# Recurrent attention feeding a gated feed-forward: x of blocks 1 to 5 kept as f32, early loads without padding rows, planner recounted

## The chip, the cores and the metric

One core of one Trainium2 chip. The metric is the device time of one execution in microseconds (us), the median over the runs; lower is better. PE is the matmul engine (TensorE), DVE the vector engine, ACT the scalar engine, POOL the GpSimd engine, and SP the engine that issues nearly all DMA transfers. L1369 is line 1369 of the kernel before.

## The reference

```python
# r, k, v, w: [4, 8, 768, 48], u: [8, 48]
for t in range(S):
    cur = einsum('bhd,bhe->bhde', u[None] * kt, vt)
    y[:, :, t] = einsum('bhd,bhde->bhe', rt, state + cur)
    state = wt[:, :, :, None] * state + einsum('bhd,bhe->bhde', kt, vt)
x = y.transpose(0, 2, 1, 3).reshape(3072, 384)
h = x @ w_in                                   # [384, 2048]
g = where(h >= 1, h, where(h <= -1, 0, (h + 1) ** 2 / 4))
return g @ w_out                               # [2048, 384]
```

A linear attention with a decaying state gives x, and a feed-forward with a quadratic gate follows. All is f32.

## The kernel before, in words

The attention is done in 12 chunks of 256 tokens (u = 0 to 11), the feed-forward in six blocks of 512 tokens, so two chunks fill the x of a block. A matmul of f32 accuracy is made of three: each operand is split into a high and a low part (type fp32r), and three of the four products are summed. The 16 slices of the weights come packed and are unpacked for the first time during block 0 (POOL takes the sign, L485; DVE and ACT the rest, L481 to L490). Blocks 3 to 5 use fewer, combined products (the lines after L1000).

A chunk, in the names of the rows. `wq` holds the decay of half the channels, two tiles to a chunk and three tiles in turn; `rk` holds r and k of the same half, also two to a chunk and three in turn (rk_81, rk_82 and rk_83 are the three; wq_78, wq_79 and wq_80 likewise). Both have 128 rows, of which 2 x 48 carry data and 2 x 16 are padding that comes with the transfer. DVE scans the decay (`p`, L550, and `y` backwards, L545) and multiplies r and k by the scans (L571, L621). In the first three chunks (u < EARLY) ACT forms u*k (`nk`, L561), with u in four columns of the constants `cst`. PE multiplies r with u*k and with k inside groups of 32 tokens (`among`, L591, whose results DVE picks by a mask, L597), transposes k (L630), forms the update of the state (`umat`, L660; DVE adds it, L676 to L681), and puts y together in two runs of matmuls, `cross` and `along` (both L703). L591, L660 and L703 use 64x64 or 64x48 corners of the array; here they are called narrow, and the 128-row products L1369 (x @ w_in), L1389 and L1045 (g @ w_out) wide.

The result is evacuated into x. 48 data rows of 64 leave 16 free rows in each half, which the fourth part of the channels (`last`) fills by six small DMAs on SP (L827); chunks 0 and 1 do that by matmuls instead. In blocks 0 to 3 x is split while it is evacuated: ACT copies the high part (L781), DVE subtracts for the low part (L779). In blocks 4 and 5 (FLAT) ACT copies f32 into `xf` (L775), the six DMAs fill it, and `divided` splits a half block at once (ACT L1150, DVE L1152).

The order on every engine is made when the program is built. `op(engine, cost, due, reads, writes, emit)` records an operation with an assumed cost; `order()` lists them greedily by a key; `best()` tries several keys and keeps the order whose planned end is earliest; `kept_warm()` puts matmuls of zeros (`fill`, L439) where PE would idle, to hold its clock. `load` records a DMA, and `first=` fixes the place of the first ones in SP's queue.

Of the kernel before, what the change touches and what calls it, by code (L numbers as in the profile page):

```python
# [10 lines left out]
F32 = mybir.dt.float32  # L11
# [33 lines left out]
FLAT = {NB - 2, NB - 1}  # L45
# [5 lines left out]
USE, SPAN, COLUMN = 0.68, 3.4, 0.00168  # L51

EAGER, LATE = 16.0, 0.3
RISES = 7.0
COLD = 7.0
# [3 lines left out]
BACK, SHAKES, SHAKE, SEED = 4, 40, 0.7, 5  # L59
# [4 lines left out]
class Plan:  # L64
# [10 lines left out]
    BLOCK, FETCH = 256, 3.9  # L75
# [12 lines left out]
    def add(self, engine, cost, emit, due, reads=(), writes=(), port=False, size=0, fresh=True, first=None, grab=False, uses=(), drop=None, code=0):  # L88
# [6 lines left out]
        for x in writes:  # L95
# [3 lines left out]
                             fresh=fresh and engine == "PE", touch={*reads, *writes}, first=first, grab=grab, drop=drop, then=None, code=code,  # L99
# [19 lines left out]
    def best(self, steps, times):  # L119

        found = None
        for _ in range(ROUNDS):
            for op in self.ops:
                when, ahead = op["due"]
                op["key"] = times[when] - ahead
            order = self.order()
            end = max(self.end.values())
            if found is None or end < found[0]:
                found = end, order, (self.begin, self.end, self.given, self.extra)
            times = [self.begin[n] for n in steps]  # L130

        draw = random.Random(SEED)
        for n in range(SHAKES):
            if n % BACK == 0:
                self.begin, self.end, self.given, self.extra = found[2]
            for op, key in zip(self.ops, self.late()):
                op["key"] = key + draw.gauss(0.0, SHAKE) * (n % BACK == 0 < n)
            order = self.order()
            end = max(self.end.values())
            if end < found[0]:  # L140
                found = end, order, (self.begin, self.end, self.given, self.extra)
        self.begin, self.end, self.given, self.extra = found[2]
        for op in self.ops:
            op["touch"] |= {("b", self.given[n]) for n in op["uses"]}
        return found[1]
# [39 lines left out]
    def kept_warm(self, order, engine, banks, fill):  # L185

        ops, begin, end = self.ops, self.begin, self.end
        free, out, busy = 0.0, [], []
        used = {b: [n for n in order if b in ops[n]["touch"]] for b in banks}
        for n in order:  # L190
            op = ops[n]
            if op["e"] == engine:
                at = begin[n]
                use = sum(max(0.0, y - max(x, at - SPAN)) for x, y in busy)
                lack = at - free - (0.3 if at > EAGER else -LATE if free < COLD else 0.1)
                if at > EAGER:
                    lack = min(USE * SPAN - use, lack)
                if free and lack > 0.15:
                    for b in banks:
# [4 lines left out]
                            ops[m]["e"] == engine for m in (before, after)) and end[before] <= free  # L204
                        fresh = after is None or ops[after]["fresh"]
                        if held or fresh and at - max(0.0 if before is None else end[before], free) > (lack if at > EAGER else at - free - 0.3 - 1e-6):
                            out.append(lambda b=b, lack=lack, free=free, held=held: fill(b, lack, free, held))
                            busy.append((at - lack, at))
                            break
                free = at + op["cost"]  # L210
                busy.append((at, free))
            out.append(op["emit"])
        return out

    def order(self):
# [18 lines left out]
        issued = [(0, -99.0, 0.0)]  # L234

        def fetched(code):
            at = issued[-1][0] + code - self.BLOCK
            for had, t, each in reversed(issued):
                if had <= at:
                    return t + (at - had) * each + self.FETCH  # L240
            return 0.0
# [4 lines left out]
        def ready(n):  # L246
# [3 lines left out]
            if ops[n]["code"] > 64:  # L250
                t = max(t, fetched(ops[n]["code"]) - ops[n]["cost"])
# [6 lines left out]
        while any(open_.values()):  # L258
# [12 lines left out]
            assert t < never  # L271
            n = min((n for n in open_[e] if ready(n) <= t + 1e-9 and forced.get(e) in (None, n)),
# [1186 lines left out]
```

## Time and profile before

| | before |
|---|---|
| time, median of 3 runs | 501.33 us (500.96 to 502.52) |
| the profiled execution | 503.06 us, of which span 501.5 us |
| PE busy | 488.0 us, 97% of the span |
| DVE busy | 404.1 us, 81% |
| ACT busy | 312.7 us, 62% |
| POOL busy | 101.4 us, 20% |
| DMA | 54.30 MB, mean 108 GB/s |
| chain that ended last | PE 90%, DVE 4%, DMA 2%, issue 2%, ACT 1% |

The span is the recorded part of the execution; 1.56 us of the profiled execution lie around it. Busy is the time in which an engine had an instruction running. A busy PE isn't the same as a useful one: zero matmuls count too, and so do matmuls that drain slowly.

### The profile page before, as it was taken

How to read it: one execution, taken by the hardware profiler on the slowest of the kernel's cores; microseconds unless marked ns; L12 is line 12 of the kernel's file. 1: busy time of each engine (PE TensorE's matmuls, PEld its weight loads, DVE VectorE, ACT ScalarE, POOL GpSimd, SP SyncE). 2: the span in 40 equal slices, each digit the busy share in tenths (PEclk: the TensorE clock that was granted, in tenths of full speed). 3: DMA queues.
4: the chain of work that ended last, by engine and by line, in shares of the span. 5: the costliest groups of instructions: out<-in, count | busy, mean ns of one | idle time of the engine just before them, and what ended most of it. 6: DMA issues, size and time to landing. Idle time of an engine off the chain costs nothing.

```text
span 501.5 us, 13736 instructions
## 1 busy us (share of the span) xinstructions
PE 488.0 (97%) x5767; PEld 426.8 (85%) x5767; DVE 404.1 (81%) x702; ACT 312.7 (62%) x658; POOL 101.4 (20%) x80
## 2 busy tenths in 40 slices
PE   6979999999999999999999999999999999999996
PEld 4768988889999998888888788889899989898985
DVE  5899999988888898898999878779877675675573
ACT  4669799855555473765555656788866565465461
POOL 1656604530111111303031124432100000000000
PEclk9989999999999999999999999999999999999999
DMA  8984750522343434446153212222141000010002
GB/s 293 400 300 163 300 211 17 185 81 86 107 133 107 141 103 138 169 137 215 39 210 105 106 52 74 42 52 55 30 118 22 1 1 1 23 41 1 3 1 69
DMA packets 33286, 54.30 MB, mean 108 GB/s; under 512 B 15424, under 2 KB 22720, under 8 KB 33216
## 3 DMA queue, kind: packets, MB, share of 16 engines
q1 hardware_dynamic: 32784, 52.95, 31.9%
q8 instruction: 47, 0.77, 0.6%
q10 hardware_dynamic: 432, 0.39, 0.2%
q14 instruction: 23, 0.19, 0.1%
HBM read 47.04 MB, written 4.72 MB: 103 GB/s over the span
## 4 chain that ended last, share of the span: by engine, by line
PE 90%; DVE 4%; DMA 2%; issue 2%; ACT 1%; SPq 0%; DVEq 0%; ACTq 0%
PE h L1369 39%; PE acc L1389 20%; PE acc L1045 10%; PE bank L1045 9%; PE bank L703 4%; PE bank L591 3%; PE bank L630 2%; PE bank L660 1%; DMA cst<-in_consts 1%; DMA rk<-in_rk 1%; DVE fl L487 1%; PE bank L439 1%; PE acc L591 1%; DVE wt L490 1%; DVE y L545 0%
## 5 line engine op out<-in xcount | busy, mean ns | idle before, releaser
L1369 PE MATMUL h<-x,wt 128*128 128x512 f32 (+1 forms) x1035 | 220.1, 360 | 3.0 <-DVE x L779 2.9
L1369 PEld LDWEIGHTS h<-x,wt 128*128 128x128 f32 x1035 | 169.5, 189 | 31.7 <-DVE x L779 3.1
L1389 PE MATMUL acc<-gh,wt 128*128 128x256 f32 (+1 forms) x402 | 80.3, 335 | 0.0
L1389 PEld LDWEIGHTS acc<-gh,wt 128*128 128x128 f32 x402 | 60.9, 188 | 7.4
L1007 DVE SCALAR_TENSOR_TENSOR rk<-rk,h 128x512 f32<-128x512 f32 x48 | 32.8, 683 | 35.8 <-ACT rk L1006 34.2
L1178 ACT ACTIVATE g<-h 128x256 f32<-128x256 f32 (+1 forms) x67 | 31.9, 476 | 44.8 <-PE h L1369 40.6
L1004 ACT ACTIVATE rk<-h 128x512 f32<-128x512 f32 x48 | 28.6, 596 | 38.8 <-PE h L1369 38.8
L485 POOL TENSOR_SCALAR wraw<-fl 128x768 uint16<-128x768 f32 x13 | 41.8, 3224 | 51.4 <-ACT wraw L483 49.9
L1180 DVE SCALAR_TENSOR_TENSOR g<-g,h 128x256 f32<-128x256 f32 (+1 forms) x67 | 35.2, 529 | 14.4 <-ACT g L1179 12.4
L1389 PE MATMUL acc<-gl,wt 128*128 128x256 f32 (+1 forms) x201 | 44.5, 329 | 0.0
L1182 ACT CAST gh<-g 128x256 fp32r<-128x256 f32 (+1 forms) x67 | 32.7, 494 | 18.8 <-DVE g L1180 8.8
L617 POOL TENSOR_TENSOR r<-cst,d 128x512 f32<-128x512 f32 x18 | 20.2, 1143 | 99.8 <-PE bank L703 81.7
L1183 DVE TENSOR_TENSOR gl<-g,gh 128x256 fp32r<-128x256 f32 (+1 forms) x67 | 38.7, 589 | 0.8 <-ACT gh L1182 0.7
L1389 PEld LDWEIGHTS acc<-gl,wt 128*128 128x128 f32 x201 | 32.3, 188 | 4.0
L1179 ACT ACTIVATE g<-g 128x256 f32<-128x256 f32 (+1 forms) x67 | 34.4, 513 | 1.1
L550 DVE TENSOR_TENSOR_SCAN p<-wq,seeds 128x520 f32<-128x520 f32 x24 | 32.0, 1331 | 3.2 <-DMA wq<-in_w 2.3
L1006 ACT ACTIVATE rk<-rk 128x512 f32<-128x512 f32 x48 | 30.4, 634 | 0.9
L545 DVE TENSOR_TENSOR_SCAN y<-wq,seeds 128x520 f32<-128x520 f32 x24 | 29.8, 1242 | 0.8
L609 POOL TENSOR_TENSOR nk<-nk 128x768 f32<-128x768 f32 x9 | 17.3, 1920 | 61.4 <-DMA nk<-in_nk 37.9
L1013 DVE TENSOR_TENSOR gl<-rk,gh 128x512 fp32r<-128x512 f32 x36 | 25.5, 717 | 2.7 <-ACT gh L1012 2.4
L1013 DVE TENSOR_TENSOR g_again<-rk,nk_again 128x512 fp32r<-128x512 f32 x33 | 22.8, 701 | 5.8 <-ACT nk_again L1012 5.5
L1012 ACT CAST gh<-rk 128x512 fp32r<-128x512 f32 x36 | 22.1, 619 | 8.3 <-DVE rk L1007 4.7
(212 smaller groups left out, 914.5 us busy)
## 6 DMA issues: line engine op xcount, KB each, us to landing
rk<-in_rk SPq DMA_DIRECT2D x24, 512.0 KB, 5.3
wraw<-in_wbits SPq DMA_DIRECT2D x16, 768.0 KB, 7.5
nk<-in_nk SPq DMA_DIRECT2D x9, 768.0 KB, 4.7
wq<-in_w SPq DMA_DIRECT2D x24, 260.5 KB, 2.9
vn<-in_v SPq DMA_DIRECT2D x12, 384.0 KB, 6.8
last<-in_w SPq DMA_DIRECT2D x12, 256.0 KB, 3.0
out_y<-xf SPq DMA_DIRECT2D x15, 128.0 KB, 1.8
out_y<-g SPq DMA_DIRECT2D x6, 256.0 KB, 2.2
```

Source lines behind the costliest of these rows:

```text
L485: op(on, 0.62 if f in SIGNS else 3.2, due, [("fl", k)], [("raw", f)], lambda: e.tensor_scalar(out=half(1), in0=s, scalar1=0.0, scalar2=327 ...
L550: V.tensor_tensor_scan(out=pv[:, q].rearrange("p n c -> p (n c)"), data0=w[:, 0:SEG], data1=sv, initial=0.0, op0=ALU.mult, op1=ALU.add,)
L1007: op("DVE", 0.66, due, [("h", n)], [qk], lambda: V.scalar_tensor_tensor(out=gf, in0=gf, scalar=1.0, in1=bank[plan.given[hk]], op0=ALU.min, ...
L1013: op("DVE", 0.67, due, [key, ("h", i, k)], fresh_in(("l", i, k)), lambda: V.tensor_tensor(out=spare(k, 3 + i), in0=x, in1=spare(k, i).bitc ...
L1045: PE.matmul(bank[i][:, half * UT : half * UT + UT], lhsT=w[wi], rhs=g[gi], start=(b, i) not in opened, stop=True, skip_group_check=True)
L1178: op("ACT", c, due, [("h", n)], [("g", gk)], lambda: nc.scalar.activation(gs, hs(), AF.Relu, scale=0.5, bias=0.5), uses=[hk])
L1179: op("ACT", c, due, (), [("g", gk)], lambda: nc.scalar.activation(gs, gs, AF.Square))
L1180: op("DVE", 0.13 + 0.53 * k, due, [("h", n)], [("g", gk)], lambda: nc.vector.scalar_tensor_tensor(out=gs, in0=gs, scalar=1.0, in1=hs(), op ...
L1182: op("ACT", c, due, [("g", gk)], [("gh", gk)], lambda: nc.scalar.copy(ghs, gs))
L1183: op("DVE", 0.17 + 0.54 * k, due, [("g", gk), ("gh", gk)], [("gl", gk)], lambda: nc.vector.tensor_tensor(out=gls, in0=gs, in1=ghs.bitcast( ...
L1369: nc.tensor.matmul(hp, lhsT=wx[f][:, cs], rhs=xt[:, j, :], start=n == 0, stop=n == 8)
L1389: nc.tensor.matmul(o[j], lhsT=wx[f][:, cs], rhs=gt, start=first and i == 0, stop=stop and i == 2, skip_group_check=True)
```

## The change

- FLAT is now blocks 1 to 5, and `xf` stays at two tiles, taken in turn. Chunks 2 to 7 are evacuated by ACT alone, filled by six DMAs of 16 KB instead of 32 KB, and split by `divided`, which is recorded right behind the second chunk of the block.
- Early r and k (all six loads of the first three chunks) are sent as two transfers of 48 rows into tiles that DVE clears at the start (three MEMSETs of 128x1024, L541 of the new file); `wq` likewise, from the second load of a tile on.
- The four columns of u ride as two more columns of `wq` (523 instead of 521); `cst` shrinks to 128x192 and is loaded behind r and k instead of between them. `perm` is made on POOL instead of being loaded; the transfer of `us` waits for weight slice 5.
- The planner: other costs for the narrow matmuls, a price on going from narrow to wide (SWITCH) and a wish to keep narrow runs together (HOLD), an exact count of the instruction blocks that PE fetches, zero matmuls planned within the search, 12 shakes and 17 local ones (MOVES) in place of 40 shakes.

```diff
-FLAT = {NB - 2, NB - 1}
+FLAT = set(range(1, NB))
-USE, SPAN, COLUMN = 0.68, 3.4, 0.00168
+USE, SPAN, COLUMN = 0.68, 3.4, 0.00184
-BACK, SHAKES, SHAKE, SEED = 4, 40, 0.7, 5
+BACK, SHAKES, SHAKE, SEED = 4, 12, 0.7, 3
+MOVES = (521500, 587009, 888496, 283031, 12939, 164576, 355387, 922251, 331532, 701578, 205853, 500742, 732557, 367787, 559427, 662263,
...
-    xf = tiles(len(FLAT), [128, 3, WIDE], F32, "xf")
+    xf = tiles(2, [128, 3, WIDE], F32, "xf")
+    for i in range(3):
+        op("DVE", 0.6, (0, 200.0 - i), (), [("k", i), ("r", i)], lambda i=i: V.memset(rk[i], 0.0))
...
+    def rows_of(due, out, in_, keys, own, first):
+        if not own:
+            return load(due, out, in_, keys, first=first)
+        users = {n for key in keys for n in plan.readers.get(key, ())}
+        for h in range(2):
+            i = slice(HP * h, HP * h + D)
+            n = load(due, out[i], in_[i], [(*key, h) for key in keys], keys, first=first)
+            plan.ops[n]["deps"] |= users
...
-            load(due, wq[slot[q]], a["w"][u, q], [("w", slot[q])], first=rank(1 - q))
-            load(due, rk[slot[q]], a["rk"][u, q], [("k", slot[q]), ("r", slot[q])], first=rank(4 - 2 * q))
+            rows_of(due, wq[s], a["w"][u, q], [("w", s)], early and s in padded, rank(1 - q))
+            padded.add(s)
+            rows_of(due, rk[s], a["rk"][u, q], [("k", s), ("r", s)], early, rank(3 - q))
-            load(due, cst, a["consts"], ["cst"], first=3)
+            load(due, cst, a["consts"], ["cst"], first=4)
-                A.mul(ku[:, q, cs], rk[slot[q]][:, 1, cs], u_col[:, 2 * q + pr : 2 * q + pr + 1])
+                A.mul(ku[:, q, cs], rk[slot[q]][:, 1, cs], wq[slot[q]][:, SEG + 1 + pr : SEG + 2 + pr])
...
+        cost = op["cost"] + self.SWITCH * (op["small"] != was) + self.EVENT * op["code"]
...
             for u in ADDED.get(b, ()):
                 attention(u, *PULLED.get(u, (step_of(u), None)))
+                if u % 2 and u // 2 in FLAT and u // 2 < NB - 2:
+                    divided(u // 2)
```

How the orders move, at four places. First SP's queue at the start of the program, before:

```order
L419 DMA wq_78<-in_w 128x521
L419 DMA wq_79<-in_w 128x521
L419 DMA rk_81<-in_rk 128x1024
L419 DMA cst_67<-in_consts 128x196
L419 DMA rk_82<-in_rk 128x1024
L469 DMA wraw_143<-in_wbits 128x1536
L419 DMA vn_85<-in_v 128x2x384
L419 DMA below_71<-in_below 128x64
L469 DMA wraw_153<-in_wbits 128x1536
L419 DMA wq_80<-in_w 128x521
```

And the same place after the change (L529 is the line of `load` there, L579 the fetch of packed weights):

```order
L529 DMA wq_78<-in_w 128x523
L529 DMA wq_79<-in_w 128x523
L529 DMA rk_81<-in_rk 48x1024 x2
L529 DMA rk_82<-in_rk 48x1024 x2
L529 DMA cst_67<-in_consts 128x192
L579 DMA wraw_153<-in_wbits 128x1536
L529 DMA vn_85<-in_v 128x2x384
L529 DMA below_71<-in_below 128x64
L529 DMA wq_80<-in_w 128x523
L579 DMA wraw_163<-in_wbits 128x1536
```

`cst` has gone behind both tiles of r and k, and the third tile of the decay (wq_80) ahead of the second slice of weights.

DVE in the first chunk, before, from the multiplications of r and k to the first unpacking of weights:

```order
L571 TENSOR_TENSOR rk_82<-rk_82,y_87 128x512
L621 TENSOR_TENSOR rk_81<-rk_81,p_86 128x512
L621 TENSOR_TENSOR rk_82<-rk_82,p_86 128x512
L597 COPY_PREDICATED r_90<-cst_67,acc_111 128x512
L597 COPY_PREDICATED r_89<-cst_67,acc_110 128x512
L597 COPY_PREDICATED r_89<-below_71,acc_112 128x512
L597 COPY_PREDICATED r_90<-below_71,bank_115 128x512
L549 MEMSET seeds_73 128x8
L550 SCALAR_TENSOR_TENSOR p_86<-wq_80,seeds_73 128x520
L487 SCALAR_TENSOR_TENSOR fl_107<-fl_107,wraw_143 128x768
```

The same stretch after the change (order's name for the scan is SCALAR_TENSOR_TENSOR here):

```order
L701 TENSOR_TENSOR rk_82<-rk_82,y_87 128x512
L751 TENSOR_TENSOR rk_81<-rk_81,p_86 128x512
L751 TENSOR_TENSOR rk_82<-rk_82,p_86 128x512
L727 COPY_PREDICATED r_89<-cst_67,acc_110 128x512
L679 MEMSET seeds_73 128x8
L680 SCALAR_TENSOR_TENSOR p_86<-wq_80,seeds_73 128x520
L727 COPY_PREDICATED r_90<-cst_67,acc_111 128x512
L727 COPY_PREDICATED r_89<-below_71,acc_112 128x512
L727 COPY_PREDICATED r_90<-below_71,bank_115 128x512
L674 RECIPROCAL seeds_73<-p_86 128x8
```

The scan of the next chunk's decay (wq_80) has moved up between the first pick and the other three.

PE in chunk 4, before, at the end of the state's update:

```order
L660 MATMUL bank_117<-vn_85,kt_91 64x48 x2
L660 MATMUL h_114<-vn_85,kt_91 64x48 x2
L660 MATMUL bank_117<-vn_85,kt_91 64x48 x2
L660 MATMUL h_114<-vn_85,kt_91 64x48 x2
L1369 MATMUL h_113<-x_95,wt_898 128x256 x9
```

And after (L790 is `umat`, L833 `put`):

```order
L790 MATMUL bank_117<-vn_85,kt_91 64x48 x2
L790 MATMUL h_114<-vn_85,kt_91 64x48 x2
L790 MATMUL bank_117<-vn_85,kt_91 64x48 x2
L790 MATMUL h_114<-vn_85,kt_91 64x48 x2
L833 MATMUL bank_115<-rk_81,st_93 64x64
L833 MATMUL bank_116<-rk_81,st_93 64x64
```

`along` now follows `umat` with no wide product between them. The same holds in chunks 0, 1, 7 and 10; over the whole program the narrow runs that are followed by a wide product go from 39 to 34, and from 31 to 28 behind the first 60 us. Ahead of the first L721 no fill is left, and all fills together go from 22 rows with 5736 columns to 12 rows with 3509.

ACT behind the evacuation of chunk 3 (the second half of block 1), after the change (L1308, L1309 and L1312 are parts of the gate, L1280 the copy of `divided`):

```order
L1308 ACTIVATE g_97<-h_113 128x256
L1309 ACTIVATE g_97<-g_97 128x256
L1280 CAST x_95<-xf_109 128x3x256
L1308 ACTIVATE g_98<-h_114 128x256
L1309 ACTIVATE g_98<-g_98 128x256
L1312 CAST gh_100<-g_97 128x256
```

In the program before, chunk 3 had no such copy: x_95 was written by L781 and L779 straight from the bank. The copy now waits for the six DMAs, with the gates of the next products queued behind it.

## Rows read from the trace of the kernel before

**Rows 1.** Busy time of each engine in stretches of the span, instructions in brackets, then the granted TensorE clock (1.00 is full), the DMA share and the rate.

```profile
0.00:10.00 10.00, 5.23 (x35) 3.28 (x36) 5.28 (x9) 3.58 (x8) 2.23 (x14) 1.00 0.78 262
10.00:20.00 10.00, 10.00 (x280) 8.33 (x278) 8.03 (x12) 5.10 (x7) 5.01 (x2) 0.83 1.04 404
20.00:30.00 10.00, 7.00 (x40) 4.71 (x34) 9.82 (x16) 7.95 (x15) 6.28 (x3) 1.00 1.01 388
...
40.00:50.00 10.00, 10.00 (x250) 9.62 (x250) 9.89 (x17) 9.55 (x24) 6.16 (x2) 1.00 0.52 187
...
60.00:100.00 40.00, 40.00 (x381) 33.57 (x380) 37.46 (x55) 35.11 (x61) 15.57 (x6) 1.00 0.44 158
100.00:300.00 200.00, 200.00 (x3087) 174.07 (x3086) 174.47 (x309) 112.44 (x276) 35.62 (x26) 1.00 0.37 121
300.00:490.00 190.00, 189.60 (x1300) 169.34 (x1300) 135.88 (x252) 123.52 (x239) 19.94 (x26) 1.00 0.12 31
```

**Rows 2.** All waits of PE in the span: line, what it waited for, total us, times, longest us (two of five).

```profile
PE h L1369 <- DVE x L779: 2.9, 1, 2.9
...
PE bank L630 <- DVE rk L571: 2.0, 1, 2.0
```

**Rows 3.** The chain of work that ended last, 1 to 31 us: start, duration, what.

```profile
2.36 5.36 DMA cst<-in_consts
...
7.81 0.92 ACT nk L561 x2
8.74 0.70 DVE rk L571
...
9.49 0.66 PE bank L630 x4
10.15 0.20 PE bank L439 x2
10.35 1.92 PE acc L591 x50
...
29.46 1.21 PE h L1369 x8
```

**Rows 4.** DVE in order of time, 1 to 21 us: start, duration, line, operation, tiles, count, and in brackets the idle time before it with its releaser.

```profile
1.58 0.07 DVE L549 MEMSET seeds<- 128x8 f32 x1 [1.58 <-POOL seeds L424]
3.97 1.24 DVE L550 TENSOR_TENSOR_SCAN p<-wq,seeds 128x520 f32<-128x520 f32 x1 [2.33 <-DMA wq<-in_w]
...
8.74 0.69 DVE L571 TENSOR_TENSOR rk<-rk,y 128x512 f32<-128x512 f32 x1 [0.61 <-ACT nk L561]
...
12.33 1.29 DVE L621 TENSOR_TENSOR rk<-rk,p 128x512 f32<-128x512 f32 x2 [0.72 <-PE acc L591]
13.54 1.33 DVE L597 COPY_PREDICATED r<-cst,acc 128x512 f32<-128x512 int32 x2
15.99 0.73 DVE L597 COPY_PREDICATED r<-below,acc 128x512 f32<-128x512 int32 x1 [1.11 <-PE bank L591]
...
17.38 1.24 DVE L550 TENSOR_TENSOR_SCAN p<-wq,seeds 128x520 f32<-128x520 f32 x1
```

**Rows 5.** Nearest rows for a MEMSET of 128x1024 on DVE: the MEMSETs of POOL (lines by shape, mean ns), and the shortest per element that DVE has (its order of time near 31 us).

```profile
L429 POOL MEMSET r<- 128x512 f32 x2 | 1.0, 524 | 0.0
...
30.71 0.53 DVE L475 CAST wt<-fl 128x768 fp32r<-128x768 f32 x1
```

**Rows 6.** The chain that ended last near chunk 3 (127 to 144 us) and near 190 us: start, duration, what.

```profile
135.78 1.05 PE h L1369 x9
...
138.38 1.25 PE h L1369 x9
...
140.68 1.56 PE bank L703 x96
...
189.03 2.10 PE h L1369 x9
191.13 1.56 PE bank L703 x96
192.69 2.29 PE h L1369 x9
```

**Rows 7.** Groups of instructions by shape, 100 to 420 us: busy us, mean ns of one, idle before. The ways in which x is evacuated and split.

```profile
L779 DVE TENSOR_TENSOR x<-bank,x 128x384 fp32r<-128x384 f32 x12 | 6.4, 550 | 2.0 <-ACT last L781 1.9
...
L1152 DVE TENSOR_TENSOR x<-xf,x 128x768 fp32r<-128x768 f32 x4 | 3.8, 950 | 0.0
...
L775 ACT COPY xf<-bank 128x384 f32<-128x384 f32 x8 | 4.0, 495 | 4.2 <-PE bank L703 4.2
...
L1150 ACT CAST x<-xf 128x768 fp32r<-128x768 f32 x4 | 3.3, 832 | 0.0
```

**Rows 8.** SP in order of time: the six fills of chunk 3 and of a later chunk (start, issue time), with the next load; and the fills into `xf` in all.

```profile
144.85 4.21 SPq L827 DMA_DIRECT2D x<-last  x6
150.55 0.33 SPq L419 DMA_DIRECT2D wq<-in_w  x1
...
252.90 1.37 SPq L827 DMA_DIRECT2D xf<-last  x1
...
255.46 4.30 SPq L827 DMA_DIRECT2D xf<-last  x5
...
DMA to landing us min/median/max: 1.7/1.9/7.8
```

More of the change, by code (lines that the diff above doesn't have):

```diff
@@ L213, in kept_warm, with pieces, records, pe_takes @@
         return out
+    def pieces(self, n):
+        out = []
+        while n >= 32:
+            out.append(min(512, n if n < 128 else n // 128 * 128))
+            n -= out[-1]
+        return out
+    def records(self, n):
+        return self.put_in[n][-1] if n in self.put_in else 0
+    def pe_takes(self, n, t, pe, between=0.0):
+        op = self.ops[n]
+        idle = self.records(n)
+        was = pe["small"] and not idle
+        cost = op["cost"] + self.SWITCH * (op["small"] != was) + self.EVENT * op["code"]
+        for code, start, span in ((idle, between, t - between), (op["code"] * (1 + self.DENSE), t, cost)):
+            past = -(pe["count"] - self.EDGE) % self.BLOCK
+            if past < code:
+                at = start + span * past / code
+                when = pe["edge"] + (self.SLOWER if at < self.BUSY else self.FETCH)
+                if start == t:
+                    cost += max(0.0, when - at)
+                pe["edge"] = max(at, when)
+            pe["count"] += code
+        pe["small"] = op["small"]
+        return cost
@@ new lines, in replay @@
+    def replay(self, order):
+        ops = self.ops
+        free, end, begin, lands = {}, {}, {}, []
+        port = bus = 0.0
+        pe = dict(count=self.LEAD, edge=-99.0, small=False)
+        for n in order:
+            op = ops[n]
+            e = op["e"]
+            t = max((end[m] + self.after(m, n) for m in op["deps"]), default=0.0)
+            if n in self.extra:
+                t = max(t, end[self.extra[n]] + self.HOPS[ops[self.extra[n]]["e"]])
+            t = max(t, free.get(e, 0.0))
+            if op["port"]:
+                t = max(t, port)
+            if op["size"] and len(lands) >= LANES:
+                t = max(t, lands[-LANES])
+            cost = op["cost"]
+            if e == "PE":
+                cost = self.pe_takes(n, t, pe, free.get(e, 0.0)) * (2 if t < RISES else 1)
+            begin[n], end[n] = t, t + cost
+            free[e] = end[n] - self.OVERLAP.get(e, 0.0)
+            if op["port"]:
+                port = free[e]
+            if op["size"]:
+                bus = max(bus, t) + op["size"] / (300e3 if t < 8.0 else 390e3)
+                end[n] = bus + 2.0
+                lands.append(end[n])
+        self.begin, self.end = begin, end
@@ L233, in order @@
         forced, given, extra = {}, {}, {}
[L234 to L241, printed above, removed]
+        pe = dict(count=self.LEAD, edge=-99.0, small=False)
         spare = [(0.0, b, None) for b in SPARE]
@@ L249, in ready @@
                 t = max(t, min(spare)[0]) if spare else never
-            if ops[n]["code"] > 64:
-                t = max(t, fetched(ops[n]["code"]) - ops[n]["cost"])
+            if ops[n]["small"]:
+                past = -(pe["count"] + self.records(n) - self.EDGE) % self.BLOCK
+                m, took = n, 0.0
+                while m is not None:
+                    code = ops[m]["code"] * (1 + self.DENSE)
+                    if past < code:
+                        when = pe["edge"] + (self.SLOWER if t < self.BUSY else self.FETCH)
+                        return max(t, when - took - ops[m]["cost"] * past / code)
+                    past, took, m = past - code, took + ops[m]["cost"], ops[m]["then"]
             return t
@@ L292, in order @@
             begin[n] = t
-            end[n] = t + op["cost"] * (2 if e == "PE" and t < RISES else 1)
+            if e == "PE":
+                cost = self.pe_takes(n, t, pe, free.get(e, 0.0)) * (2 if t < RISES else 1)
+            end[n] = t + cost
             free[e] = end[n] - self.OVERLAP.get(e, 0.0)
@@ L347 @@
 SPLITS = {2, 7}
+SPARED = set()
+SIGN, HALF = 3.2, 1.2
 SIGNS = {9, 10, 12}
@@ L488, in weight @@
             out=s.bitcast(I32), in0=s.bitcast(I32), scalar=3, in1=front(), op0=ALU.logical_shift_left, op1=ALU.bitwise_or), port=True)
[L489 removed]
+        op(*(("POOL", HALF) if f in SPARED else ("DVE", 0.48) if f in SPLITS else ("ACT", 0.83)), due, [("fl", k)], [("wh", f), ("raw", f)], split, port=f in SPLITS and f not in SPARED)
         op("DVE", 0.95, due, [("fl", k), ("wh", f)], [("wl", f)], lambda: V.tensor_tensor(
```

200 lines of the change are left out of this document (119 added, 81 removed).

## The prediction

> **What bounds the kernel now.** I read the busy time by stretches first. From 60 us on PE is never idle: 40.00 of 40, 200.00 of 200 and 189.60 of 190 us [rows 1]. DVE fills 174 of the 200 us from 100 to 300, ACT 112, so both have room there. Before 60 us it is the other way round: DVE is busy 9.82 of 10 us from 20 to 30 and 9.89 from 40 to 50, while PE has 7.00 in the former [rows 1], and some of what it does is zero matmuls. So the kernel has two parts: a front that lasts as long as DVE's work in it, and a packed PE behind it. The list of PE's waits says the same: its only long ones are for DVE, 2.9 us for the first x and 2.0 for the first transposes [rows 2]. An edit is therefore worth something if it takes time out of DVE's row in the front, or columns or drains out of PE's row behind it, and nothing if it only frees DVE or ACT after 60 us.
>
> The chain shows how the front begins: the constants land at 7.72 (2.36 + 5.36), ACT multiplies k by u, DVE takes rk*y at 8.74, PE transposes and multiplies inside the groups until 12.27 [rows 3]. DVE's row has three holes on that way: 0.61 ahead of 8.74 for ACT, 0.72 ahead of 12.33 for PE, 1.11 ahead of 15.99 for PE. The scan of the third tile of decay then ends at 17.38 + 1.24 = 18.62 [rows 4], and from there DVE runs without a hole worth the name.
>
> **The change part by part.**
>
> *Clearing rk on DVE.* Three MEMSETs of 1024 columns, new on DVE. No such row exists. By POOL's MEMSET, 524 ns for 512 columns, one costs 1.05; by DVE's shortest, the CAST of 768 columns in 0.53, one costs 0.71 [rows 5]; by its pick of 512 columns, 1.33 for two or 0.67 each, one costs 1.33 [rows 4]. I take 1.05, the same operation. The first row of DVE waits 1.58 for POOL [rows 4], which these three needn't; beginning near 1 us (an estimate), they end at 1 + 3.15 = 4.15. The first scan would start there plus a hop, 4.25 instead of 3.97: **+0.3**, from 0 at the short end to +1.1 at the long one. Behind them on SP rk's own transfers wait, of which the first are issued at about 2 and 3 us, so nothing is lost there at 1.05.
>
> *Constants behind rk, no padding rows, u beside the decay.* ACT waited for the constants until 7.72. Now it needs wq and rk only. Ahead of the second tile of rk stand 2 x 0.39 MB where 2 x 0.52 + 0.10 MB stood; the 0.36 MB less are 1.4 us at the 262 GB/s of the first 10 us [rows 1]. I count on 1.0, so ACT has both products with u by about 8.9. PE's order then runs the first L721 ahead of both transposes, from 9.1, and at 1.92 us [rows 3] it is through at 11.1. DVE loses its 0.61 hole, so rk*y starts at 8.74 - 0.61 + 0.3 = 8.4; from there to the end of the second rk*y it took 12.33 - 0.72 - 8.74 = 2.9 [rows 4], which makes 11.3. Both meet: rk*p starts at 11.4 instead of 12.33, **-0.9**.
>
> *The scan between the picks.* The hole of 1.11 ahead of the picks with `below` [rows 4] is where the scan of the next decay now stands (1.24). The third decay tile is now the ninth transfer and has about 0.8 MB of weights less ahead of it: at 404 GB/s [rows 1] 2 us sooner. So the hole goes: **-1.1**. Together rk*p to the end of scan and picks takes 18.62 - 12.33 - 1.11 = 5.2, ending at 16.6 instead of 18.62: -2.0. I carry **-1.8** into the packed part, because the few small holes up to 60 us hang on POOL and PE and not on where DVE began. Bounds: 0 if something else is late in the front, -3 if the new order also packs the rest of it (fewer zero matmuls, 5736 columns down to 3509, say only that it means to). The second half of the first x moves back in DVE's order, behind the first rk*p of the next chunk; that costs its product about 0.8 of the gain at 29.46 [rows 3], but DVE does other needed work meanwhile.
>
> *Narrow runs.* Nine wide matmuls of 256 columns take 1.05; behind `umat` 1.25 (138.38). With 512 columns it is 2.10 and 2.29 behind L703 (192.69) [rows 6]. So every narrow run that a wide product follows costs 0.20. Behind 60 us there are three fewer: **-0.6**, from 0 to -0.8.
>
> *x of blocks 1 to 3 as f32.* For each of chunks 2 to 7, DVE loses two subtractions of 0.55 and two smaller ones and gains one of 0.95; ACT gains a copy of 0.83 and the f32 copy costs what the fp32r one did [rows 7]. That is some 0.7 us less on DVE and 0.8 more on ACT per chunk, all behind 60 us, where ACT is 56% busy and PE never waits for either [rows 1]: **0** on the end. Without that cover it would be 6 x 0.8 = 5 us. What can hurt is the longer way to x: evacuation, six fills, the copy, the subtraction, where fill and both parts used to go side by side. The tight place is chunk 3: by the new order PE has nine groups of 1.05 between `along` and the first product that needs it, 9.65 with the 0.20. The way there: 1.6 for the four evacuations (2 x 0.50 and two small ones [rows 7]), then the fills, whose issue takes 4.21 and the last landing some 1.3 behind it (1.9 from the start of its own issue of 0.6) [rows 8], 5.5; the copy 0.83, the subtraction 0.95, hops 0.3: 9.2. It fits, by 0.4.
>
> *The rest* (loading `us` later, `perm` on POOL, the blocks of instructions counted) touches no row on the path: 0.
>
> **Sum:** -1.8 - 0.6 = -2.4. The profiled execution was 503.06 = 501.5 of span and 1.56 around it, so 500.7 for one like it. The runs' median lies 1.7 lower, at 501.33; the forecast on it is **498.9**.
>
> **A rule against it.** Splitting one transfer of 128 rows into two of 48 is what the Trainium skill's page "SBUF — State Buffer" advises against ("Can I just issue two DMAs to hit both halves?": "No."): a transfer reaches all ports only if it spans all 128 partitions, and two halves run one after the other. Its section "Door 1: The DMA port swizzle" gives 196 GB/s where 128 partitions get 328; by an estimate from that ratio, 0.6, the forecast would be near 500. No run here shows a large transfer of 48 rows.
>
> **The rivals.**
>
> *The front's gain is lost; no change.* The mechanism by rows: if 48-row transfers move at half the 262 GB/s [rows 1], the 0.79 MB of rk take 6.0 instead of 3.0 us; then rk's second tile lands near 10.6, ACT is through at 11.5, PE at 13.6, and rk*p starts at 13.7, 1.4 later than before. With the 1.1 hole closed and the narrow runs this gives 501.33 + 1.4 - 1.1 - 0.6 = 501.0. The rule named above is one reason to think so. MEMSETs at the long end, or a longer stretch at the lower clock between 10 and 20 us (0.83 granted on average there [rows 1], so one part at 1.2 GHz) cost 0.8 to 1.5 of the gain as well. 499.8 to 501.3, about 500.5. Against it: the ring was busy for 0.78 of the first 10 us only, and half as many bytes in padding go.
>
> *More gain.* The front's remaining zero matmuls show slack on PE; if the reordered decoding of weights lets PE pack two or three us earlier: 495.8 to 497.4. Against it: DVE has no holes left there, and it loses no work in the front.
>
> *Slower: x of chunk 3 late.* The fills of one later chunk took from 252.90 to 259.76 to issue alone, with a load between them, and one landed 7.8 us behind its issue [rows 8]. With 6.9 + 1.9 = 8.8 in place of 5.5 the way is 12.5 against 9.65: PE stops for 2.9, and ACT holds the next gates behind the waiting copy. That gives 501.8, and 502.9 or more if a second chunk meets it or the front's gain fails too. It decides as soon as the fills take over 6 us at chunk 3. For it: the margin is 0.4. Against it: before, chunk 3's own fills had twice the bytes, and SP's order ahead of them is nearly the same.
>
> **How the numbers follow.** About 0.3%, 1.5 us, is what a measurement of this kernel tells from no change: faster is below 499.8, slower above 502.8. Likeliest (497.4 to 499.8, 498.9): 0.50. More gain: 0.16. Front lost: 0.22. Chunk 3 late: 0.12, half of it above 502.8. The range leaves out a tail of the second and most of the last: 496.2 to 501.4. Faster is 0.50 + 0.16 = 0.66; slower 0.07 with a rest for the unforeseen; same 0.27.
>
> **What would show it.** Right: three MEMSETs on DVE near 1 us each that end about 4.2; rk*p near 11.4; no hole of a microsecond on DVE between 11 and 20, its second pick with `below` done by 17; PE without waits from about 58 us; 1.25 instead of 1.05 in 28 places behind 60 us. Wrong: rk landing behind 9 us; a wait of the products L1500 for DVE's subtraction L1282 of x near 140; holes on DVE for POOL or ACT between 20 and 60.

## The result, and the profile after

The changed kernel takes 504.95 us (median of five runs, 504.11 to 506.64) against 501.33: a ratio of 1.0074, with a 95% interval of 1.0048 to 1.0100. It is 3.6 us slower, where 2.4 us less were forecast. The profiled execution took 504.11 us with a span of 502.6. It is the shortest of its runs, while the one shown of before (503.06) is longer than the three it stands beside. So the two traces differ by 1.1 us where the medians differ by 3.6: sizes are taken below from ratios of medians, and places from the traces.

The stretches of the changed kernel, columns as in [rows 1]:

```profile
10.00:20.00 10.00, 9.08 (x272) 7.56 (x273) 9.38 (x15) 6.10 (x13) 6.28 (x5) 1.00 1.04 326
20.00:30.00 10.00, 8.18 (x88) 5.12 (x89) 9.12 (x14) 7.25 (x14) 4.29 (x2) 0.85 1.06 254
...
60.00:100.00 40.00, 40.00 (x485) 32.79 (x485) 38.77 (x57) 35.28 (x63) 15.45 (x6) 1.00 0.51 178
100.00:300.00 200.00, 196.95 (x3075) 171.58 (x3073) 168.42 (x292) 113.64 (x276) 36.66 (x26) 1.00 0.36 117
300.00:490.00 190.00, 190.00 (x1298) 169.54 (x1298) 135.85 (x248) 125.01 (x240) 20.20 (x26) 1.00 0.12 31
```

Three things differ from [rows 1]. The last column: from 10 to 20 us 326 GB/s where 404 were moved, from 20 to 30 us 254 for 388, with the DMA engines just as busy (1.04 and 1.06). Then PE from 100 to 300 us: 196.95 where it was 200.00. And the granted clock, a mean over time at 1.2 and at 2.4 GHz: before it was low from 10 to 20 us (0.83), now from 20 to 30 (0.85), behind the stop of PE near 24 (PE is busy 3.69 of the 5 us from 20 to 25, and the clock is 0.70 from 25 to 30). With whole transfers (below) it is 1.00 in both stretches; what the low clock costs apart from the late weights isn't measured. The longest waits of PE tell of the first two places:

```profile
PE acc L721 <- ACT nk L691: 5.6, 1, 5.6
...
PE h L1500 <- DVE g L1310: 1.9, 2, 1.0
PE bank L721 <- ACT nk L691: 1.8, 1, 1.8
...
PE bank L833 <- ACT kt L769: 0.8, 1, 0.8
```

The first is at the start, where no zero matmuls stand any more ahead of the first L721, and is no loss by itself. The 1.8 us are near 24 us, where ACT waits 1.90 us for r and k of the next chunk:

```profile
24.96 0.91 ACT L691 ACTIVATE nk<-rk,wq 128x256 f32<-128x256 f32 x2 [1.90 <-DMA rk<-in_rk]
```

The waits for the gate (L1310) and for kt (L769) lie behind 60 us, where before PE had one wait of 0.4 us.

The beginning of the front went nearly as forecast. DVE, rows as in [rows 4]:

```profile
1.26 0.91 DVE L541 MEMSET rk<- 128x1024 f32 x1 [1.26 <-PEq L1571]
...
4.44 1.24 DVE L680 TENSOR_TENSOR_SCAN p<-wq,seeds 128x520 f32<-128x520 f32 x1
...
12.00 1.29 DVE L751 TENSOR_TENSOR rk<-rk,p 128x512 f32<-128x512 f32 x2 [0.42 <-PE acc L721]
...
14.00 1.24 DVE L680 TENSOR_TENSOR_SCAN p<-wq,seeds 128x520 f32<-128x520 f32 x1
...
16.37 0.72 DVE L727 COPY_PREDICATED r<-below,bank 128x512 f32<-128x512 int32 x1
```

The hole of 1.11 is gone, and scan and picks end at 16.37 + 0.72 = 17.1 instead of 18.6: 1.5 us of the 2.0 are there. What happened next stands in the chain of work that ended last:

```profile
12.76 9.88 DMA vn<-in_v
...
24.56 8.94 DMA wraw<-in_wbits
...
33.58 0.91 ACT fl L593
...
35.93 0.44 ACT kt L769
...
36.41 0.38 PE bank L866
```

Between 12.76 and 33.5 us the chain runs over transfers: SP waits for the landing of one before it can issue the next, the fifth slice of weights is issued at 24.56 and lands 8.9 us later, ACT waits for it, and the copy of kt that PE needs stands behind it on ACT. Before, no transfer stood in the chain behind 7.72 until the one that is issued at 44.01 and lands at 48.

### The profile page after: what moved, and what is told of

Its sections match the earlier page's. It is cut to its first block, busy times and chain, and to the rows that moved or that the text cites. A ratio compares the mean times of both kernels' runs of the same rounds, so it can differ in the third digit from the quotient of the medians.

```text
span 502.6 us, 13679 instructions
## 1 busy us (share of the span) xinstructions
PE 481.4 (96%) x5747; PEld 421.5 (84%) x5747; DVE 403.7 (80%) x687; ACT 318.0 (63%) x664; POOL 103.6 (21%) x84
## 4 chain that ended last, share of the span: by engine, by line
PE 85%; DMA 7%; DVE 3%; issue 1%; ACT 1%; SPq 1%; ACTq 0%; DVEq 0%
PE h L1500 39%; PE acc L1520 18%; PE acc L1175 10%; PE bank L1175 9%; PE bank L833 4%; DMA vn<-in_v 3%; PE bank L721 2%; DMA wraw<-in_wbits 2%; PE bank L760 1%; DMA rk<-in_rk 1%; PE bank L790 1%; DVE p L680 1%; DMA xf<-last 1%; DVE y L675 1%; SPq L529 1%
## 5 line engine op out<-in xcount | busy, mean ns | idle before, releaser
L1500 PE MATMUL h<-x,wt 128*128 128x512 f32 (+1 forms) x1035 | 219.2, 359 | 2.5 <-DVE g L1310 1.9
L1500 PEld LDWEIGHTS h<-x,wt 128*128 128x128 f32 x1035 | 168.4, 188 | 31.1 <-DVE g L1310 2.7
L1520 PE MATMUL acc<-gh,wt 128*128 128x256 f32 (+1 forms) x402 | 80.2, 335 | 0.0
L1520 PEld LDWEIGHTS acc<-gh,wt 128*128 128x128 f32 x402 | 60.9, 188 | 7.5
L1308 ACT ACTIVATE g<-h 128x256 f32<-128x256 f32 (+1 forms) x67 | 31.8, 476 | 42.9 <-PE h L1500 39.7
L1310 DVE SCALAR_TENSOR_TENSOR g<-g,h 128x256 f32<-128x256 f32 (+1 forms) x67 | 35.1, 528 | 18.0 <-ACT g L1309 17.3
L1520 PE MATMUL acc<-gl,wt 128*128 128x256 f32 (+1 forms) x201 | 44.5, 329 | 0.0
L1312 ACT CAST gh<-g 128x256 fp32r<-128x256 f32 (+1 forms) x67 | 33.1, 495 | 15.1 <-DVE g L1310 9.3
L1313 DVE TENSOR_TENSOR gl<-g,gh 128x256 fp32r<-128x256 f32 (+1 forms) x67 | 36.1, 548 | 0.2 <-ACT gh L1312 0.2
L1520 PEld LDWEIGHTS acc<-gl,wt 128*128 128x128 f32 x201 | 32.3, 188 | 4.0
L1309 ACT ACTIVATE g<-g 128x256 f32<-128x256 f32 (+1 forms) x67 | 34.1, 513 | 1.1
L675 DVE TENSOR_TENSOR_SCAN y<-wq,seeds 128x520 f32<-128x520 f32 x24 | 32.0, 1332 | 0.8
```

The lines of the kernel that those rows point to most:

```text
L675: V.tensor_tensor_scan(out=y_[:, ::-1], data0=w[:, SEG:0:-1], data1=sv[:, ::-1], initial=0.0, op0=ALU.mult, op1=ALU.add)
L1309: op("ACT", c, due, (), [("g", gk)], lambda: nc.scalar.activation(gs, gs, AF.Square))
L1310: op("DVE", 0.13 + 0.53 * k, due, [("h", n)], [("g", gk)], lambda: nc.vector.scalar_tensor_tensor(out=gs, in0=gs, scalar=1.0, in1=hs(), op ...
L1312: op("ACT", c, due, [("g", gk)], [("gh", gk)], lambda: nc.scalar.copy(ghs, gs))
L1313: op("DVE", 0.17 + 0.54 * k, due, [("g", gk), ("gh", gk)], [("gl", gk)], lambda: nc.vector.tensor_tensor(out=gls, in0=gs, in1=ghs.bitcast( ...
L1500: nc.tensor.matmul(hp, lhsT=wx[f][:, cs], rhs=xt[:, j, :], start=n == 0, stop=n == 8)
```

## The experiments

Kernels of one group ran on one chip together with the kernel before; between groups the ratio to the kernel before is compared. The groups are again, whole, nofill and whole_nofill; cols, halves64, whole_noclear and whole_flat45; whole2, noclear2, whole_tuned and whole_nonk; whole3, cols2 and whole_nkdve. All but whole_flat45 keep the changed kernel's order on PE, DVE and ACT, apart from the instructions named.

**The transfers or the fills.** First the changed kernel again.

> The changed kernel once more, for a second trace. Three theories of why it is 3.6 us slower. Split: the 48-row transfers of r, k and decay move fewer GB/s (10 to 30 us: 350, 302, 247, 260 against 410, 398, 402, 373 before), so the weight slices land 2 to 5 us late and the front loses its gain. Fills: the copy of divided waits on ACT for the six fills with gates behind it, and PE stops behind 60 us (1.0 at 215). Order: the new order of the planner itself is slower, whatever is loaded. All three expect 504 to 506 here, with the stop of PE near 215 again; whether other stops come and go from run to run is what this trace adds.

Measured: 505.47 us, ratio 1.0063 (1.0039 to 1.0088). From 10 to 20 and 20 to 30 us it moved 327 and 236 GB/s.

In `whole` the pair of 48-row transfers is sent as one of 128 rows:

```diff
-            plan.ops[n]["deps"] |= users
+            plan.ops[n].update(deps=plan.ops[n]["deps"] | users,
+                emit=(lambda: nc.sync.dma_start(out=out, in_=in_)) if h == 0 else (lambda: None))
```

> Each early pair of 48-row transfers is sent as one transfer of 128 rows at the place of the first; all engines but SP keep the order of the changed kernel, the clearing stays. Split: the rate from 10 to 30 us returns to about 390 GB/s although more bytes are sent, the fourth to sixth weight slice land 2 to 4 us sooner (near 25, 30 and 33 us), the time falls by 2 to 4 us to 501 to 503. Fills, Order: the front's bytes matter little, less than 0.7 us either way.

Measured: 501.20 us, ratio 0.9985 (0.9971 to 0.9999), 4.3 us less than the changed kernel beside it. The stretches of whole from 10 to 30 us:

```profile
10.00:20.00 10.00, 9.54 (x249) 7.96 (x242) 9.80 (x15) 6.23 (x11) 6.56 (x2) 1.00 1.04 403
20.00:30.00 10.00, 8.02 (x152) 5.38 (x151) 9.88 (x14) 7.63 (x15) 6.67 (x3) 1.00 1.03 403
```

The rate is back at 403 GB/s, though a third more bytes of r and k are sent. What that does to ACT's unpacking (L593) is seen in its order of time. The changed kernel, fourth and fifth slice:

```profile
28.55 0.91 ACT L593 ACTIVATE fl<-wraw 128x768 f32<-128x768 f32 x1 [0.67 <-DMA wraw<-in_wbits]
...
33.58 0.91 ACT L593 ACTIVATE fl<-wraw 128x768 f32<-128x768 f32 x1 [0.97 <-DMA wraw<-in_wbits]
```

And whole:

```profile
24.76 0.98 ACT L593 ACTIVATE fl<-wraw 128x768 f32<-128x768 f32 x1
...
30.28 0.93 ACT L593 ACTIVATE fl<-wraw 128x768 f32<-128x768 f32 x1 [0.64 <-DVE wt L602]
```

The slices are unpacked 3.8 and 3.3 us sooner, and the wait is one for DVE again, not for a transfer. So the split transfers are the main cause of the loss. The theory that the new order alone is slower than the old one falls: with whole transfers it is level. It isn't the 2.4 us faster that were forecast either.

`nofill` leaves out the fills of chunks 2 to 7, `whole_nofill` does both:

```diff
-                   lambda e=e, h=h, j=j: fill(e, h, j), size=16384 * parts_x)
+                   (lambda: None) if u in (2, 3, 4, 5, 6, 7) else (lambda e=e, h=h, j=j: fill(e, h, j)), size=16384 * parts_x)
```

> The changed kernel without the six fill transfers of chunks 2 to 7, so the fourth part of the channels of x is missing in blocks 1 to 3; the order on all engines but SP is kept. Fills: the copy of divided no longer waits 3.1 us near 212, the stop of PE there (1.0) and smaller ones go, 1 to 2 us less than the changed kernel. Split, Order: 0 to 0.7 less.

> Both edits at once (again without the fourth part of the channels of x in blocks 1 to 3). Split and Fills together: the two gains add to 3 to 5 us, 500 to 502, level with the kernel before or better. Order: it stays within 1 us of the changed kernel.

Measured: nofill 504.74 us, 1.0056 (1.0035 to 1.0078), 0.7 below again; whole_nofill 500.80, 0.9975 (0.9962 to 0.9989), 0.4 below whole. Each difference is within the intervals, so the fills' price is at most small in the total. Where it is paid, the trace of the changed kernel shows on ACT:

```profile
215.43 0.83 ACT L1280 CAST x<-xf 128x768 fp32r<-128x768 f32 x1 [3.10 <-DMA xf<-last]
...
217.80 0.58 ACT L769 COPY kt<-bank 128x512 f32<-128x512 f32 x1
```

and on PE:

```profile
121.01 2.25 PE L1500 MATMUL h<-x,wt 128*128 128x256 f32 x17 [1.02 <-DVE g L1310]
...
218.43 0.70 PE L833 MATMUL bank<-rk,st 64*64 64x64 f32 x32 [0.82 <-ACT kt L769]
...
264.22 2.13 PE L1500 MATMUL h<-x,wt 128*128 128x512 f32 x8 [0.88 <-DVE g L1310]
```

The copy of `divided` for chunk 6 waits 3.10 us for its fills; it isn't the copied x that PE then lacks (no product waits for x), but kt, whose copy is queued behind it. The stop is 0.82 us, and it isn't at chunk 3, where it was looked for. Without the fills it goes from both traces. That alone shows little, since with the fills the same stop is 0.3 in whole, 0.6 in whole3 and absent in whole2. The two other stops stay; they are DVE's.

**Why a pair is slow: its rows or its number.** `cols` sends each pair as two transfers of 128 rows with half the columns, `halves64` as rows 0 to 63 and 64 to 127. Both carry the bytes of whole and the number of transfers of the changed kernel. For cols (for r and k, the first transfer holds r and the second k):

```diff
-            plan.ops[n]["deps"] |= users
+            c = (slice(h, h + 1) if len(out.shape) == 3 else slice(0, 262) if h == 0 else slice(262, 523)); plan.ops[n].update(deps=plan.ops[n]["deps"] | users, emit=lambda c=c: nc.sync.dma_start(out=out[:, c], in_=in_[:, c]))
```

and for halves64 (HP is 64):

```diff
-            plan.ops[n]["deps"] |= users
+            plan.ops[n].update(deps=plan.ops[n]["deps"] | users, emit=lambda h=h: nc.sync.dma_start(out=out[HP * h : HP * h + HP], in_=in_[HP * h : HP * h + HP]))
```

> Why are the pairs slow? Each early pair is sent as two transfers of all 128 rows with half the columns each (padding rows included, as many bytes as whole, as many transfers as the changed kernel). Theory rows: a transfer is slow because its rows lie in one half of the partitions; then this one is fast, 10 to 30 us at 390 to 410 GB/s, 501 to 502. Theory count: two transfers instead of one cost the rate, by their number or by places in SP's queue; then the rate stays at 250 to 300 from 15 to 30 us and the time at 504 to 506.

> Each early pair is sent as rows 0 to 63 and rows 64 to 127, whole width (as many bytes as whole). Theory rows: slow, and slower than the changed kernel because a third more bytes go at the low rate: 220 to 300 GB/s from 10 to 30 us, 505 to 508. Theory count: as the changed kernel or a little above, 504 to 506. A third theory, padding: the transfers are slow because 48 rows aren't a full half; then this one is fast, 501 to 502.

> Two transfers of all rows and half the columns each, now beside whole on one chip. Rows alone: level with whole within 0.5 us. Rows and count: the rate is that of whole but the doubled number of transfers in SP's queue makes the fifth weight slice 1 to 2 us later (31.4 against 29.3 in the earlier traces): 1 to 2.5 us above whole.

> Whole transfers a third time, beside the other two on one chip: 0.998 to 1.000 of the kernel before.

Measured: cols 503.37, ratio 1.0023 (1.0001 to 1.0046); halves64 509.28, 1.0128 (1.0088 to 1.0167); in a later group cols2 503.37, 1.0025 (1.0010 to 1.0040), beside whole3 501.87, 0.9998 (0.9981 to 1.0015). The stretches from 10 to 30 us of cols2:

```profile
10.00:20.00 10.00, 9.54 (x266) 7.74 (x262) 8.76 (x13) 5.70 (x10) 6.55 (x4) 1.00 1.04 390
20.00:30.00 10.00, 8.47 (x103) 5.86 (x107) 9.84 (x15) 7.74 (x14) 5.51 (x3) 1.00 1.05 394
```

and of halves64:

```profile
10.00:20.00 10.00, 9.28 (x230) 7.59 (x233) 7.77 (x12) 6.29 (x11) 5.46 (x5) 1.00 1.04 317
20.00:30.00 10.00, 5.65 (x118) 4.43 (x113) 7.61 (x11) 4.98 (x10) 1.74 (x1) 0.85 1.04 276
```

As many transfers and bytes, and DMA engines as busy (1.04 and 1.05), but 276 GB/s against 394, and against 388 in cols on the chip of halves64: the rows decide the rate. The theory of padding falls too, since with 64 full rows the kernel is slower than with 48 (more bytes at the low rate).

The number is another matter. cols2 stays 1.5 us above whole3 beside it (1.0025 against 0.9998, with intervals that just overlap), and cols has the same ratio on another chip. But the traces don't show this loss in the front. What PE gets done by 60 us of the wide matmuls, L1500 (x @ w_in) and L1520 (g @ w_out) in turn, is in cols2

```profile
0.00:60.00 60.00, 13.77 (x94) 12.07 (x95) 1.00 0.76 275
0.00:60.00 60.00, 9.42 (x72) 8.82 (x72) 1.00 0.76 275
```

and in whole3

```profile
0.00:60.00 60.00, 14.46 (x97) 12.62 (x98) 1.00 0.74 275
0.00:60.00 60.00, 9.46 (x72) 8.86 (x72) 1.00 0.74 275
```

That is 94 + 72 = 166 matmuls in cols2, as in cols, and 169 in whole3. All kernels with whole transfers and this order have 165 (whole_nkdve, below) to 171 (whole), the two traces of the changed kernel 154 and 135, halves64 has 113. What is longer in cols is the end of the program. DVE's last row is in cols2 and in whole3

```profile
496.58 0.42 DVE L1248 TENSOR_TENSOR xf<-bank,xf 128x256 f32<-128x256 f32 x1 [0.62 <-PE bank L1175]
...
494.24 0.42 DVE L1248 TENSOR_TENSOR xf<-bank,xf 128x256 f32<-128x256 f32 x1 [0.62 <-PE bank L1175]
```

and the span ends at 503.3 and 498.9: 6.3 us behind the end of that row in cols2 and 4.2 in whole3, likewise 6.1 in cols, and 4.4 and 4.2 in whole and whole2. No transfer of r, k or decay runs there. So no trace shows a price of the number in the front; the end is seen in one execution of each run only, and why it is longer stays open. cols also halves what a transfer brings to a row; that wasn't tried apart from the number.

**The clearing, and x of blocks 1 to 3.** `whole_noclear` drops the three MEMSETs from whole; `whole_flat45` sets FLAT back, after which the planner makes another order.

```diff
-        op("DVE", 0.6, (0, 200.0 - i), (), [("k", i), ("r", i)], lambda i=i: V.memset(rk[i], 0.0))
+        op("DVE", 0.6, (0, 200.0 - i), (), [("k", i), ("r", i)], lambda: None)          # whole_noclear
-FLAT = set(range(1, NB))
+FLAT = {NB - 2, NB - 1}                                                                  # whole_flat45
```

> Whole transfers and no clearing of rk on DVE. The clearing puts the first scan at 4.44 instead of 3.97 and holds the first transfer of rk on SP by 0.3 us. If that is carried to the end, 0.3 to 0.5 less than whole: 500.7 to 501.0. If the front waits for transfers and ACT there anyway, no difference to whole (within 0.3).

> Whole transfers without the clearing on DVE once more, now beside whole. It measured 1.0015 on another chip. Theory clearing helps (by holding rk's transfers back behind the decay's): 1 to 2 us above whole here too. Theory chip: within 0.5 us of whole.

> Whole transfers, and x of blocks 1 to 3 split at its evacuation again as in the kernel before (FLAT is blocks 4 and 5); the planner makes its order anew, so single stops of PE may come and go. Theory flat costs: ACT's copy that waits for the fills (stop of 1.0 near 212) goes, 0.5 to 1.5 less than whole, 499.7 to 500.7. Theory flat gains: DVE has 4 us more to do between 100 and 300 and its scans delay gates more often, 0.5 to 2 more than whole, 501.7 to 503. Theory neutral: within 0.5 of whole.

> The kernel with whole transfers once more, beside the three below on one chip. It was 501.2 with a ratio of 0.9985 to the kernel before; if that is the kernel and not the chip, again 0.997 to 1.000.

Measured: whole_noclear 503.17, 1.0015 (0.9992 to 1.0038); later noclear2 502.80, 1.0019 (0.9997 to 1.0041), beside whole2 501.93, 1.0001 (0.9987 to 1.0016). Without the clearing it is not faster; the median is 0.9 us above whole beside it (noclear2), and the ratio of the earlier group is 1.0 us above the mean of whole (0.9995), with intervals that overlap. The front isn't slower (167 and 166 wide matmuls by 60 us, counted as above); again the end is longer, 5.6 and 5.7 us behind DVE's last row, and why is open. whole_flat45: 503.58, 1.0018 (0.9992 to 1.0045), so the flat x is not what costs: undone, the kernel is level with whole or slower. Its order is another one, so this doesn't price the flat x alone.

**The stops behind 60 us.** `whole_tuned` moves the load of nk (768 KB), which stood behind the first of chunk 6's fills, behind the last of them. `whole_nonk` leaves POOL's product per token out. The lines that matter in whole_tuned:

```diff
+                if min(js) < i < max(js):
...
+                    order.insert(max(js) + 1, n)
+                    del order[i]
```

Here i is the place of nk's load on SP and js are those of the fills of a chunk. For whole_nonk:

```diff
-            op("POOL", 2.0, due, (), ["nk"], lambda: G.tensor_tensor(
-                out=nk[:, :, 0, :], in0=nk[:, :, 0, :], in1=nk[:, :, 1, :], op=ALU.mult), port=True)
+            op("POOL", 2.0, due, (), ["nk"], lambda:
+                None, port=True)
```

> Whole transfers, and where the load of nk stands between the fills of a chunk on SP it is moved behind the last of them (once, near 207). If the stop of PE near 213 comes from fills that queue behind nk's 768 KB, ACT's copy starts some 3 us sooner and the stop (0.5 to 1.0) goes: 0.5 to 1.0 less than whole. If the fills are late because of the three loads ahead of nk, the copy moves less than 1 us and the time stays.

> Whole transfers, and POOL's product of r and k per token (L739) is left out, so the own-token term of chunks 3 to 11 is wrong. Theory POOL: the stops of PE near 117 and 257 (about 1 us each, for DVE's gate behind two scans) come from DVE's instructions being stretched while POOL runs L739 (a scan of 2.45 or 2.75 for 1.24); without it both go, 1.5 to 2 less than whole. Theory order: the scans stand ahead of the gate and that alone is too late; then the stops stay at 0.5 or more each.

Measured: whole_tuned 503.25, 1.0032 (1.0013 to 1.0051), slower than whole2 by 1.3. ACT in that trace (L1294 is the copy of `divided` there, L1322 the gate):

```profile
210.59 0.84 ACT L1294 CAST x<-xf 128x768 fp32r<-128x768 f32 x1
214.83 0.60 ACT L1322 ACTIVATE g<-h 128x512 f32<-128x512 f32 x1 [3.41 <-DMA out_y<-g]
```

The copy no longer waits. But nk's load now stands ahead of the stores of g, and ACT's next gate, which writes into g, waits 3.41 us for those. The wait went to another row of ACT, and the copy of kt that stands behind it comes later than before (L847 and L783 are `put` and the copy of kt there):

```profile
217.73 0.69 PE L847 MATMUL bank<-rk,st 64*64 64x64 f32 x32 [1.75 <-ACT kt L783]
```

PE's stop for kt is 1.75 us, where it is 0 to 0.6 in the traces of whole.

whole_nonk: 500.24, 0.9964 (0.9949 to 0.9979), 1.7 less than whole2, and PE's two stops for DVE's gate (near 117 and 257 in the expectation) are gone from its trace. How POOL comes into DVE's gate is seen in the changed kernel near 118 us, on POOL:

```profile
117.33 2.21 POOL L739 TENSOR_TENSOR nk<-nk 128x768 f32<-128x768 f32 x1 [1.95 <-DMA nk<-in_nk]
```

and on DVE:

```profile
118.19 2.45 DVE L675 TENSOR_TENSOR_SCAN y<-wq,seeds 128x520 f32<-128x520 f32 x1
120.56 0.39 DVE L1310 SCALAR_TENSOR_TENSOR g<-g,h 128x256 f32<-128x256 f32 x1
```

The scan, which takes 1.24 at 4.44 and in most other places, takes 2.45 while POOL runs, the gate behind it comes 1.2 us late, and PE stops for 1.02 ahead of 121.01. In the traces without the product (whole_nonk and whole_nkdve) that scan takes 1.24. The Trainium skill, "SBUF — State Buffer", section "Who interferes with whom", says that a DVE instruction with two SBUF inputs contends with a GpSimd one that reads SBUF; by that rule the scan, with two inputs, has to wait, and the trace agrees (2.45 for 1.24).

Last, the same product moved to DVE, with nothing left out: `whole_nkdve`.

```diff
-            op("POOL", 2.0, due, (), ["nk"], lambda: G.tensor_tensor(
-                out=nk[:, :, 0, :], in0=nk[:, :, 0, :], in1=nk[:, :, 1, :], op=ALU.mult), port=True)
-            op("DVE", 0.94, due, ["us"], ["nk"], lambda: V.tensor_tensor(
+            op("POOL", 2.0, due, (), ["nk"], lambda:
+                None, port=True)
+            op("DVE", 0.94, due, ["us"], ["nk"], lambda: V.tensor_tensor(out=nk[:, :, 0, :], in0=nk[:, :, 0, :], in1=nk[:, :, 1, :], op=ALU.mult) and None or V.tensor_tensor(
                 out=nk[:, :, 0, :], in0=nk[:, :, 0, :], in1=u_sb.unsqueeze(1).broadcast_to([128, 2, DM]), op=ALU.mult), port=True)
```

> Whole transfers, and the product of r and k per token (L739) is made on DVE, right ahead of the product with u (L741) that follows it; all is computed. DVE gets 9 x 0.95 us more, POOL 9 x 2 less. Theory POOL: the stops near 117 and 257 go as they did without L739, DVE isn't stretched, 1 to 2 us less than whole: about 500.5, ratio 0.996 to 0.998. Rival: DVE is tight enough there that its own 0.95 per chunk delays the gates as the stretching did: level with whole.

Measured: 500.62 us against 502.44 of the kernel before and 501.87 of whole3 beside it, ratio 0.9965 (0.9952 to 0.9979). PE's waits behind 60 us in that trace, all of them:

```profile
PE bank L833 <- ACT kt L769: 0.6, 1, 0.6
PE bank L833 <- ACT look L879: 0.2, 1, 0.2
PE h L1500 <- DVE st L808: 0.2, 1, 0.2
```

No product waits for a gate any more. This version, with whole transfers and no POOL product beside the scans, is 0.35% faster than the kernel before, and its interval (0.9952 to 0.9979) lies clear of that of whole3 (0.9981 to 1.0015).

## Why the prediction was wrong

*The step that failed* is "constants behind rk, no padding rows". It priced the new transfers by their bytes (0.36 MB less, 1.4 us sooner) at the rate of rows with 128-row transfers [rows 1]. The bytes were less and the rate fell by more: 254 GB/s for 388 between 20 and 30 us. It also looked at the first pair only. There, too, r and k came late: ACT waits for the second tile until 9.39, and "rk landing behind 9 us" was named as a sign of being wrong. But by SP's order the pairs of chunks 1 and 2 lie among the weights, and there they delay everything queued with them; the loss is not at 10 us but at 28 to 36 us, in weights that weren't touched by the change.

*Its size*, by the runs, as shares of 501.33: the changed kernel lies at 1.0068 (mean of 1.0074 and 1.0063), whole at 0.9995 (mean of three). So the split by rows cost 3.7 us; cols, at 1.0024, has a longer end and no front slower than those with whole transfers. From whole to whole_nkdve (0.9965) POOL's product cost another 1.5. The changed kernel is 5.9 us above the forecast by this mean; the last 0.7 stay open.

*The front's gain* of 1.8 can be estimated from what PE got done by 60 us. Before the change it was 126 wide matmuls (81 of L1369, 45 of L1389) and 384 of `among` (L591). In the kernels after it, those of `among` (L721) are 256. A wide matmul costs 0.117 (nine in 1.05), and 64 of `among` take 1.09 in the chain of before, so 128 of them 2.2. By that, the three traces of whole (169 to 171) are 2.8 to 3.1 us ahead of before at 60 us, and the two of the changed kernel (154 and 135) are 1.1 ahead and 1.1 behind. So the gain is there with whole transfers and was lost with the split ones. The one trace of before is 1.7 us longer than its median, so its front may be that much better than this says.

*The rival that had it right* is the second, "the front's gain is lost", but its price of 501.0 was nearly four us short, because it also stopped at the first 0.79 MB and had no stops behind 60 us. The rule weighed against the change, from the Trainium skill's "SBUF — State Buffer" ("Can I just issue two DMAs to hit both halves?" and "Door 1: The DMA port swizzle"), is borne out: between 20 and 30 us, with 128-row weights among them in both, halves64 moves 276 GB/s where cols2 moves 394, a ratio of 0.70; the page's two figures, for single transfers, give 0.6. The estimate near 500 that was made from it carried the same mistake of scope.

*The other terms.* Clearing: 0.91 per MEMSET in the rows, but 1.08 from start to start (1.26 to 2.34), where 1.05 was taken; the first scan came at 4.44 for 4.25 forecast. First chunk: rk*p at 12.00 for 11.4, so -0.3 instead of -0.9, ACT's second products with u waiting 0.76 for the second tile. The scan between the picks: the 1.1 hole closed as forecast. Narrow runs: the cost of 0.2 per run is in this trace too (1.25 for the nine of L1500 at 139.73, right behind L833). But counted in the two traces from 60 us on, the places where something else follows a narrow run go from 29 to 28 and not from 31 to 28, so that only 0.2 of the 0.6 can lie there. Three stops of 1.02, 0.82 and 0.88 that weren't there before exceed it; the prediction expected no waits of PE from about 58 us on. I had looked for new waits only where x is read. They came where an instruction of another engine is queued behind something that got longer: a gate behind a scan on DVE, kt behind a waiting copy on ACT. The term of 0 for x as f32 held but for that: no product waits for x, and DVE and ACT absorb the rest.

*What holds of the mechanism:* with whole transfers and the POOL product out of the way, nearly the same order of work gives 0.9965 of the kernel before, 499.6 on its median (498.9 to 500.3 by the interval), against the 498.9 that were forecast for the change. That the two are near is in part luck: the forecast has no term for POOL's product, and the narrow runs gave less than was put down for them. The kernel before with the product on DVE wasn't tried; PE waits only 0.4 us there behind 60 us, so little of the gain can be had in it.

## What to carry to other kernels

Price a transfer by the rows that it reaches and not by its bytes alone, and follow its price through the whole queue: whoever is next in it pays. Dropping padding rows was a bad trade here, because it made one transfer of 128 rows into two of 48. When a packed engine gains in one place, look on every engine whose results it needs for what stands ahead of them in the queue; here, moving one load turned a wait of 3.10 us into one of 3.41 at another instruction of the same engine, while taking POOL's product away from beside DVE's scans removed two stops. And where a variant is slower, look in its trace for where: the 1.5 us of cols look like a matter of the transfers that it was made to test, and its traces show them at the end of the program.

## What the runs showed of the hardware

Between 20 and 30 us the DMA engines are loaded throughout (DMA share 1.01 to 1.06). There, transfers of 48 or 64 rows among others bring the whole rate down to 236 to 276 GB/s (again 236, nofill 237, the changed kernel 254, halves64 276), against 386 to 405 with 128 rows. As many transfers as in pairs, but of 128 rows, keep the rate (cols 388, cols2 394). A POOL product of 128x768 f32 that reads SBUF stretched a DVE scan from 1.24 to 2.45 us. A MEMSET of 128x1024 f32 on DVE reads 0.91 in the profile, and the next one starts 1.07 to 1.08 after it.
